# Lists of instruction order and PSUM banks in the place of a list scheduler, in an adaLN transformer block on one core

## The chip, the cores and the metric

The program is one transformer block with adaptive layer norm and runs on one core of a Trainium2 chip. Five engines of the core have queues of their own and run beside one another: TensorE (PE, matmuls; its weight loader is shown as PEld), VectorE (DVE), ScalarE (ACT), GpSimd (POOL), and SyncE (SP), which here only issues DMA transfers. An instruction runs when those ahead of it on its engine are done and the semaphores that it waits for have been raised. TensorE writes into PSUM, eight banks of 512 float32 values by 128 partitions; everything else lies in SBUF. The metric is the device time of one execution in microseconds (us), as the median of several runs.

## The reference

```python
x = A_x                                                # [1, 2048, 1024], bf16
sa, ca, ga, sb, cb, gb = split(_silu(c) @ w_mod, 6)    # w_mod [1024, 6144]
h = _layernorm(x) * (1 + ca) + sa
q = (h @ wq).reshape(1, 2048, 32, 32).transpose(0, 2, 1, 3)   # 32 heads of 32
k, v = h @ wk, h @ wv                                         # one k and one v, [1, 2048, 32]
p = _softmax(einsum('bhqd,bkd->bhqk', q, k) * 32 ** -0.5)
o = einsum('bhqk,bkd->bhqd', p, v)
x = x + ga * (merge_heads(o) @ wo)
h = _layernorm(x) * (1 + cb) + sb
x = x + gb * ((_silu(h @ w1) * (h @ w3)) @ w2)         # w1, w3 [1024, 3584], w2 [3584, 1024]
```

## The kernel before

**Work and stages.** The 2048 tokens are cut into 8 blocks of 256. A *unit* is one block with one group of four heads, so there are 64 units; each takes 8 *steps* over the keys, 256 keys a step, 512 steps in all. A step (`s_exp`, L1257) is one score group on TensorE, eight matmuls that use 32 rows of the array each (`S<-QT,KT`, the keys against the queries of four heads), into four of the six score banks S6 (banks 0 to 5), and two exponentials on ScalarE (`U<-S`), which write one slot of the ring U (10 slots). When a unit's eight steps are done, its 64 matmuls with V (`PB<-U,V`, `av`, L1355, with 32 columns of the array each) sum the values; VectorE adds the probabilities in pairs (`PS<-U`, `PS<-PS`), and a few matmuls with a matrix of ones (`PB<-PS,ONES`) turn these sums into the softmax denominators. The rest of TensorE's work uses the full array: the projections of q, k and v, the output product with wo, and the feed-forward network of each block.

**The feed-forward network.** A block has 14 *slabs* of 256 hidden columns (`slab`, L1495). A slab is two accumulation groups of 16 matmuls, one against w1 and one against w3; ScalarE evicts the first with a tanh into TS, VectorE makes the gated product from it and from the second into HHT. Each slab needs two loads of 512 KB, one of w1 and one of w3, which go into one of three slots (`W13SL`, `slab_dma`, L1480): slots 0 and 1 lie in the tile W, slot 2 in the tile HT, so the names `PB<-QT,W` and `PB<-QT,HT` say which slot a slab reads (and `S<-QT,W`, `S<-QT,HT` where its group stands in a score bank, see below). Then come four *quarters* (`quarter`, L1532) of w2, 56 matmuls each (`PB<-W2S,HT`), with a gated residual sum into X and a store. The network and the output product of block n run among the attention steps of block n+1; those of the last block run after the attention. The start of the program has the modulation vectors, the layer norm of the 16 token tiles (`ln_stats`, L1026; the tile ST takes the statistics, XN or XNB the normalised tile), k, v and the first q.

**What sets the order.** The kernel first writes down a graph: 7,193 nodes, each one operation or a small group of matmuls, made by `op` (L55) with what it reads and writes. Edges follow from these. (All instructions are replayed through one helper, so in the profile all have the line L22.) The accumulation groups are sessions (`Sess`, L25); each needs one PSUM bank from its first matmul until its last eviction. Two banks, 6 and 7, serve them during attention; the six score banks are added as they come free at the end (`later`).

`Placer` (L564) then schedules the graph. Again and again it takes, over all engines, the node that can start first by its own clock, which runs on the durations written in the graph. Among the nodes of an engine that could start within a small slack it takes the one with the least due time `vt`. To a due time it adds an offset by kind and engine; slack, offsets and a few switches stand in the table PLAN, one row for each 8 score groups. A session takes whichever bank comes free first. `emit` (L741) turns a node into instructions and gives it the semaphore waits that its edges need, leaving out those that an earlier wait implies.

The core of the choice:

```python
for st, n in cand:
    if st <= m + slack or (n.mode == "S" and st <= m + late):
        ...
        k = (n.vt + off.get(n.tag + "/" + n.alts[0][0] if n.tag else "", 0) + (1e5 if back else 0.0), st, n.i)
        if best is None or k < best[0]:
            best = (k, st, n)
```

Each engine's instructions leave in the order of this schedule. SP's loads too: a load of a slab waits on SP until the last matmul that reads its slot is done, and the loads behind it on SP wait with it.

Of the kernel before, what the change touches and what calls it, by code (L numbers as in the profile page):

```python
# [42 lines left out]
class Graph:  # L43
# [63 lines left out]
    def alias(self, new, old):  # L107
# [7 lines left out]
PLAN = [  # L115
    (0.15, 0.06, 0.0, 1, 2.5,
     {"-/pe": -103, "-/act": -50, "-/sp": 3, "an/dve": 282, "av/dve": -1, "k/pe": -256, "k/dve": -10, "kb/pe":
      -34, "kb/dve": 65, "ln/pe": -40, "ln/act": -38, "ln/dve": -35, "ln/pool": -168, "mc/dve": -131, "mc/sp":
      108, "mod/pe": 152, "mod/dve": -37, "out/sp": -203, "pair/dve": 33, "q/pe": -5, "q/dve": 85, "q/sp": 102,
      "quarter/pe": 283, "quarter/dve": -115, "quarter/sp": -6, "s/pe": -111, "s/act": 268, "slab/pe": -5,  # L120
      "slab/act": -109, "slab/dve": -124, "slab/sp": -92, "v/pe": 334, "v/dve": -2, "v/pool": 65, "wo/pool": 36,
      "wo/sp": 49}),
    (0.05, 0.0, 0.02, 1, 0.5,
     {"-/pe": -121, "-/dve": 5, "-/pool": 99, "an/dve": 28, "av/pe": -78, "av/dve": 293, "k/pe": -7, "k/dve": 5,
      "kb/pe": -3, "kb/dve": -7, "ln/pe": -135, "ln/act": -119, "ln/dve": 218, "ln/pool": 78, "mc/pe": -52,
      "mc/dve": -88, "mc/sp": 27, "mod/pe": -3, "mod/dve": -58, "pair/dve": 15, "q/pe": -194, "q/dve": 14,
      "quarter/dve": 169, "s/pe": -109, "s/act": 7, "sc/dve": -11, "slab/pe": -47, "slab/act": -3, "slab/dve":
      -201, "slab/sp": 35, "v/pe": 32, "v/dve": -164, "v/pool": 298, "wo/pe": -1, "wo/dve": 18, "wo/pool": 11,
      "wo/sp": 3}),
    (0.3, 0.16, 0.1, 0, 3.1,  # L130
     {"-/pe": -93, "-/act": 12, "-/dve": -31, "-/pool": -31, "an/dve": 150, "av/pe": 7, "av/dve": 140, "k/pe":
      32, "k/dve": 90, "kb/pe": 2, "kb/dve": -29, "ln/pe": -31, "ln/act": -6, "ln/dve": 351, "ln/pool": -30,
      "mc/pe": -4, "mc/dve": -69, "mc/sp": -137, "mod/dve": 45, "out/sp": -162, "pair/dve": 66, "q/dve": 67,
      "quarter/pe": -36, "quarter/sp": 1, "s/pe": -112, "s/act": 140, "sc/dve": -32, "slab/pe": 146, "slab/act":
      -146, "slab/dve": -120, "slab/sp": -5, "v/pe": 131, "v/pool": -72, "wo/dve": 100, "wo/pool": -3}),
    (0.12, 0.06, 0.3, 0, 3.0,
     {"-/pe": 23, "-/act": -86, "-/dve": -4, "an/dve": 63, "av/pe": -29, "av/dve": 40, "k/pe": 4, "kb/dve": -10,
      "ln/pe": -27, "ln/act": 2, "ln/pool": 220, "mc/pe": 152, "mc/dve": 120, "mc/sp": -35, "mod/pe": -220,
      "mod/dve": -16, "out/sp": -16, "q/dve": 7, "q/sp": -147, "quarter/pe": -153, "quarter/dve": -41,
      "quarter/sp": -39, "s/pe": 23, "s/act": 1, "sc/dve": 74, "slab/pe": -18, "slab/dve": 2, "slab/sp": 30,  # L140
      "v/pe": -5, "v/dve": 35, "v/pool": 168, "wo/pool": 2, "wo/sp": -85}),
    (0.12, 0.24, 0.1, 1, 0.8,
     {"-/pe": -90, "-/act": 54, "-/dve": -67, "-/pool": 131, "an/dve": 109, "av/pe": 17, "av/dve": -135,
      "k/dve": 56, "kb/dve": 4, "ln/pe": -27, "ln/act": 1, "ln/pool": -16, "mc/pe": 4, "mc/dve": 10, "mc/sp":
      -8, "mod/dve": -44, "out/sp": -171, "q/pe": -226, "q/dve": -34, "q/sp": -3, "quarter/pe": 37,
      "quarter/dve": 416, "quarter/sp": -122, "s/pe": 145, "s/act": 282, "sc/dve": -18, "slab/pe": 96,
      "slab/act": -104, "slab/dve": 17, "slab/sp": 60, "v/pool": 23, "wo/pe": -24, "wo/dve": -41, "wo/pool":
      -164, "wo/sp": -28}),
    (0.12, 0.2, 0.02, 1, 3.2,
     {"-/pe": 9, "-/act": 22, "-/dve": -30, "-/pool": 14, "an/dve": 85, "av/pe": -38, "av/dve": -130, "k/pe": 8,  # L150
      "k/dve": 63, "kb/dve": 1, "ln/pe": -5, "ln/act": 96, "ln/dve": 351, "ln/pool": -16, "mc/pe": -3, "mc/dve":
      -18, "mc/sp": -3, "mod/pe": 2, "mod/dve": -44, "out/sp": -301, "pair/dve": -20, "q/pe": -94, "q/dve": 65,
      "q/sp": -7, "quarter/pe": 74, "quarter/dve": 413, "quarter/sp": 5, "s/pe": 204, "s/act": 233, "sc/dve": 9,
      "slab/pe": 91, "slab/act": -185, "slab/dve": -46, "slab/sp": 109, "v/pe": -238, "v/pool": 21, "wo/pe":
      152, "wo/dve": -41, "wo/pool": -168}),
    (0.12, 0.24, 0.1, 1, 3.0,
     {"-/pe": -31, "-/act": -14, "-/dve": -102, "-/pool": 64, "an/dve": 82, "av/pe": -6, "av/dve": 45, "k/pe":
      8, "k/dve": -141, "kb/dve": 25, "ln/pe": 20, "ln/act": -6, "ln/dve": -26, "mc/pe": -24, "mc/dve": 11,
      "mc/sp": -1, "mod/dve": -323, "out/sp": -145, "pair/dve": -133, "q/pe": -377, "q/dve": 7, "q/sp": -120,
      "quarter/pe": -44, "quarter/dve": -73, "quarter/sp": 5, "s/pe": 253, "s/act": 174, "sc/dve": 14,  # L160
      "slab/pe": 160, "slab/act": -109, "slab/dve": -216, "v/pe": -127, "v/pool": 1, "wo/pe": 51, "wo/dve": 14,
      "wo/pool": 47, "wo/sp": -14}),
    (0.15, 0.1, 0.0, 0, 2.6,
     {"-/pe": -17, "-/act": -69, "-/dve": -18, "-/pool": 34, "-/sp": -218, "an/dve": -166, "av/pe": -66,
      "av/dve": -19, "k/dve": 2, "kb/pe": 5, "kb/dve": -14, "ln/pe": -2, "ln/act": 6, "ln/dve": -14, "mc/pe":
      -57, "mc/dve": -128, "mc/sp": 152, "mod/pe": 56, "mod/dve": -240, "out/sp": -39, "q/pe": -36, "q/dve":
      -159, "q/sp": -155, "quarter/pe": -28, "quarter/dve": -6, "s/pe": 272, "s/act": 34, "sc/dve": 14,
      "slab/pe": -98, "slab/act": -33, "slab/dve": 13, "slab/sp": 89, "v/pe": -96, "v/pool": 191, "wo/pe": 168,
      "wo/dve": -77, "wo/sp": -8}),
    (0.15, 0.03, 0.1, 1, 2.6,  # L170
     {"-/pe": -16, "-/act": -51, "-/dve": -18, "-/pool": -118, "-/sp": -70, "an/dve": -32, "av/pe": 65,
      "av/dve": -89, "k/pe": 8, "k/dve": -133, "kb/dve": 16, "ln/pe": 69, "ln/act": -29, "ln/dve": -47, "mc/pe":
      -167, "mc/dve": 12, "mc/sp": -82, "mod/pe": -87, "mod/dve": -293, "out/sp": -51, "pair/dve": 208, "q/pe":
      -17, "q/dve": -76, "q/sp": 22, "quarter/pe": -25, "quarter/dve": 30, "quarter/sp": 10, "s/pe": 357,
      "s/act": -68, "sc/dve": 36, "slab/pe": -3, "slab/act": -68, "slab/dve": -150, "slab/sp": 263, "v/pe": 178,
# [385 lines left out]
]  # L561


class Placer:  # L564

    SWITCH = {"F": 0.105, "S": 0.111, "A": 0.1155}
    LAT = {("dve", "pe"): 0.12, ("act", "pe"): 0.1, ("act", "dve"): 0.06}
    SEM = 0.06
    SPAN = 8
# [1164 lines left out]
```

## Time and profile before

| | |
|---|---|
| runs, us | 1131.63, 1131.49, 1130.08 (median 1131.49) |
| the profiled execution, span, us | 1129.6 |
| instructions in it | 34,462 |
| bytes moved by DMA | 209.45 MB, mean 185 GB/s |
| exponentials, busy us, mean of one | 1024, 961.7, 1154 ns |
| pair sums PS<-U on VectorE | 248, 300.9 us, 1218 ns |
| loads of w1 and w3, 512 KB each | 150 into W and 74 into HT, 5.0 us each to landing (median) |

The span runs from the first to the last instruction that the profiler recorded. The time of a run holds some launch work besides. Busy times of one engine can overlap in the records (an exponential's mean of 1154 ns is longer than the distance from one to the next), so the prediction counts from start to start where it needs a price.

In groups of the profile a line reads: engine, operation, output tile <- input tiles, partitions x elements, count; then busy us, mean ns, and idle time ahead of them with what ended it. A line of the waits reads: the waiting instruction, what released it, then the idle us, the count, and the longest one. In the timeline the two first numbers are start and duration in us, and a bracket at the end is idle time ahead of the group with its releaser. In the stretches each engine has its busy us and its number of instructions.

### The profile page before, as it was taken

The page shows a single profiled execution, that of the slowest core. Times are in us where ns is not written, and L with a number is a line of the kernel's source. Part 1 is how long each engine was busy: PE and PEld are TensorE (multiplying, and loading weights), DVE is VectorE, ACT ScalarE, POOL GpSimd, SP SyncE. Part 2 cuts the span into 40 slices and gives each one's busy share as a digit, 9 for nine tenths or more (in the row PEclk, how much of TensorE's full clock was granted, in tenths as well). Part 3 has the DMA queues.
Part 4 walks back from the last instruction along what each step waited for, and adds up shares of the span by engine and source line. Part 5 has one row for each costly group of instructions (what it writes and reads, how often), then busy time and mean ns, then how long its engine had stood idle before and what let it go on. Part 6 is the DMA issues. An engine that isn't in the chain of part 4 may idle for free.

```text
span 1129.6 us, 34462 instructions
## 1 busy us (share of the span) xinstructions
PE 1110.8 (98%) x15472; PEld 753.3 (67%) x15472; DVE 976.4 (86%) x1484; ACT 1017.2 (90%) x1155; POOL 51.5 (5%) x95
## 2 busy tenths in 40 slices
PE   8999999999999999999999999999999999999998
PEld 6643445666577766777577766776577756776887
DVE  7877899999899989998999899988999899987542
ACT  6899999999999999999999999999999999984110
POOL 4100000000000001000100001000100001000000
PEclk9999999999999999999999999999999999999999
DMA  9500368665697656865696577865597568677794
GB/s 345 184 2 2 113 184 225 192 183 164 141 245 203 190 141 179 243 192 155 151 269 192 166 184 179 237 193 155 129 274 207 157 172 209 195 223 217 222 249 154
DMA packets 374307, 209.45 MB, mean 185 GB/s; under 512 B 17552, under 2 KB 365968, under 8 KB 374160
## 3 DMA queue, kind: packets, MB, share of 16 engines
q1 hardware_dynamic: 373728, 207.11, 66.3%
q8 instruction: 122, 2.00, 0.8%
q14 instruction: 25, 0.20, 0.1%
q10 hardware_dynamic: 432, 0.13, 0.0%
HBM read 199.89 MB, written 4.19 MB: 181 GB/s over the span
## 4 chain that ended last, share of the span: by engine, by line
PE 73%; ACT 22%; DVE 2%; DMA 1%; issue 0%; SPq 0%; POOL 0%
PE PB L22 55%; ACT U L22 21%; PE S L22 19%; DMA W<-in_A_wq_dram 1%; ACT HT L22 1%; DVE ST L22 1%; DVE PS L22 1%; DVE HT L22 0%; SPq L22 0%; ACT XNB L22 0%; DVE KT L22 0%; DVE XNB L22 0%; POOL RS L22 0%; DVE QT L22 0%; DVE X L22 0%
## 5 line engine op out<-in xcount | busy, mean ns | idle before, releaser
L22 ACT ACTIVATE U<-S 128x1024 bf16<-128x1024 f32 x1024 | 961.7, 1154 | 7.2 <-PE S L22 5.1
L22 DVE TENSOR_TENSOR PS<-U 128x2048 bf16<-128x2048 bf16 x248 | 300.9, 1218 | 34.1 <-ACT U L22 30.9
L22 DVE TENSOR_TENSOR PS<-PS 128x1024 bf16<-128x1024 bf16 x304 | 268.3, 883 | 4.8
L22 PE MATMUL PB<-QT,W 128*128 128x256 bf16 x1824 | 226.7, 273 | 0.0
L22 PE MATMUL S<-QT,KT 32*128 32x256 bf16 x4096 | 203.7, 273 | 6.8 <-ACT U L22 3.3
L22 PEld LDWEIGHTS PB<-QT,W 128*128 128x128 bf16 x1824 | 167.5, 98 | 45.7 <-issue 27.6
L22 PE MATMUL PB<-W2S,HT 128*128 128x256 bf16 x1512 | 187.5, 273 | 0.0
L22 PEld LDWEIGHTS PB<-W2S,HT 128*128 128x128 bf16 x1512 | 138.2, 98 | 39.4 <-issue 23.6
L22 PEld LDWEIGHTS S<-QT,KT 32*128 32x128 bf16 x4096 | 60.8, 92 | 141.6 <-ACT U L22 137.7
L22 PE MATMUL PB<-U,V 128*32 128x256 bf16 x4096 | 132.3, 273 | 0.6 <-DVE QT L22 0.6
L22 PE MATMUL PB<-QT,HT 128*128 128x256 bf16 x928 | 117.0, 273 | 0.0
L22 PEld LDWEIGHTS PB<-U,V 128*32 128x32 bf16 x4096 | 105.7, 97 | 12.9 <-issue 8.0
L22 PE MATMUL PB<-HT,W 128*128 128x256 bf16 (+1 forms) x576 | 103.3, 320 | 1.1 <-DVE QT L22 0.5
L22 PEld LDWEIGHTS PB<-QT,HT 128*128 128x128 bf16 x928 | 85.4, 98 | 22.7 <-issue 13.3
L22 DVE SCALAR_TENSOR_TENSOR HT<-HT,PB 128x512 bf16<-128x512 bf16 x100 | 68.4, 684 | 18.0 <-ACT HT L22 17.6
L22 ACT ACTIVATE HT<-PB 128x512 bf16<-128x512 f32 (+1 forms) x102 | 71.4, 701 | 9.0 <-PE PB L22 8.2
L22 PEld LDWEIGHTS PB<-HT,W 128*128 128x128 bf16 x576 | 50.2, 98 | 38.8 <-issue 14.6
L22 DVE TENSOR_TENSOR HT<-HT,PB 128x512 bf16<-128x512 bf16 x100 | 68.2, 682 | 4.3 <-PE PB L22 3.1
L22 ACT ACTIVATE HT<-S 128x512 bf16<-128x512 f32 (+1 forms) x16 | 11.1, 702 | 59.7 <-PE S L22 59.6
L22 POOL TENSOR_SCALAR RS<-MV 128x1 f32<-128x1 f32 x32 | 14.2, 445 | 968.8 <-DVE MV L22 968.8
L22 PE MATMUL PB<-WO,QT 128*128 128x512 bf16 x224 | 55.4, 381 | 0.0
L22 PEld LDWEIGHTS PB<-WO,QT 128*128 128x128 bf16 x224 | 18.8, 97 | 24.6 <-issue 7.2
(119 smaller groups left out, 699.4 us busy)
## 6 DMA issues: line engine op xcount, KB each, us to landing
W<-in_B_w_dram SPq DMA_DIRECT2D x150, 512.0 KB, 5.0
W2S<-in_B_w_dram SPq DMA_DIRECT2D x28, 1792.0 KB, 8.3
HT<-in_B_w_dram SPq DMA_DIRECT2D x74, 512.0 KB, 5.0
W2S<-in_w_mod_dram SPq DMA_DIRECT2D x8, 1024.0 KB, 7.4
X<-in_A_x_dram SPq DMA_DIRECT2D x8, 512.0 KB, 6.6
out_dram<-X SPq DMA_DIRECT2D x7, 512.0 KB, 9.6
U<-in_B_w_dram SPq DMA_DIRECT2D x1, 3584.0 KB, 18.3
W2S<-in_B_w_dram SPq DMA_DIRECT2D x1, 3584.0 KB, 12.7
```

What stands on the lines that cost most here:

```text
L22: return getattr(e, call[0])(*call[1], **call[2])
```

## The change

The class `Placer` and the table PLAN go. In their place stand ORDER, which has for each of the five engines a list of all node numbers in the order in which they are to be issued, and BANKS, a string with one digit for each session, its PSUM bank, in the order in which the sessions are created in the graph. A class `Ordered` walks the five lists. It issues an engine's next node when all nodes that it depends on have been issued (issued in the walk, that is: this is no clock) and, for the first matmul of a session, when its bank has been given back. There are no costs, no due times and no choice left. The graph, its durations and due times, the emission of waits and the rest of the kernel are as before.

```diff
-PLAN = [
-    (0.15, 0.06, 0.0, 1, 2.5,
-     {"-/pe": -103, "-/act": -50, "-/sp": 3, "an/dve": 282, "av/dve": -1, "k/pe": -256, "k/dve": -10, "kb/pe":
...
-class Placer:
...
+    "pool": """
+        0-2 61-62 70 92 63 71-72 93 144 94 101-103 82 153 145 154 146 155 88 164-166 173-175 3 192 184 193 185 202-203
...
+BANKS = (
+    "7767776667767676667767676776776667676767676767676767676667766676776766777767667766766767777667667676"
...
+class Ordered:
+
+    def __init__(self, g, banks, later, order, bank_of):
...
+        self.order = {}
+        for e, text in order.items():
+            ids = self.order[e] = []
+            for t in text.split():
+                a, _, b = t.partition("-")
+                ids += range(int(a), int(b or a) + 1)
...
+        self.free = {b: () for b in banks}
+        self.later = dict(later)
+        self.bank_of = bank_of
 
     def run(self):
...
+        for s, b in zip(seen.values(), self.bank_of):
+            s.bank = int(b)
...
         while left:
...
+            for e, ids in self.order.items():
+                while at[e] < len(ids):
+                    n = nodes[ids[at[e]]]
+                    if not all(p.done for p in n.preds):
+                        break
+                    s = n.sess
+                    if s is not None and id(s) not in opened:
+                        if s.bank in self.later and all(u.done for u in self.later[s.bank]):
+                            self.free[s.bank] = tuple(self.later.pop(s.bank))
+                        prev = self.free.get(s.bank)
+                        if prev is None:
+                            break
+                        opened.add(id(s))
+                        self.free[s.bank] = None
+                        for p in prev:
+                            n.preds.setdefault(p, False)
+                        s.prev = prev
+                    at[e] += 1
...
+                    self.emit(n, e, next(f for a, f, _ in n.alts if a == e))
...
-    pl = Placer(G, (6, 7), later, PLAN)
+    pl = Ordered(G, (6, 7), later, ORDER, BANKS)
```

What the lists move shows in the two orders of instructions. At three places they read as follows, a line a run of like instructions with its output tile, its input tiles, its shape, and how many stand in a row.

SP at the start of the program, before the change: X and W2S take token tiles, U takes pieces of w_mod for the first two modulation vectors, W takes the first 512 KB of wq.

```order
L22 DMA X<-in_A_x_dram 128x2x1024 x2
L22 DMA U<-in_w_mod_dram 128x6x1024
L22 DMA X<-in_A_x_dram 128x2x1024
L22 DMA U<-in_w_mod_dram 128x2x1024
L22 DMA W2S<-in_A_x_dram 128x2x1024
L22 DMA W<-in_A_wq_dram 128x8x256
L22 DMA U<-in_w_mod_dram 128x6x1024
L22 DMA W2S<-in_A_x_dram 128x2x1024
```

SP at the start, after the change:

```order
L22 DMA X<-in_A_x_dram 128x2x1024 x3
L22 DMA U<-in_w_mod_dram 128x6x1024
L22 DMA U<-in_w_mod_dram 128x2x1024
L22 DMA W<-in_A_wq_dram 128x8x256
L22 DMA W2S<-in_A_x_dram 128x2x1024 x2
L22 DMA U<-in_w_mod_dram 128x6x1024
L22 DMA U<-in_w_mod_dram 128x2x1024
```

The third load of X now stands ahead of the first long load of w_mod, the load of wq ahead of the first token load of W2S, and the second token load of W2S ahead of the second long load of w_mod.

TensorE in the middle of attention, around the 266th of the 512 score groups (W2S with HT is a quarter of the network), before:

```order
L22 MATMUL S<-QT,KT 128x256 x8
L22 MATMUL PB<-PS,ONES 32x256 x4
L22 MATMUL PB<-U,V 32x256 x64
L22 MATMUL S<-QT,KT 128x256 x8
L22 MATMUL PB<-W2S,HT 128x256 x12
```

The same place after:

```order
L22 MATMUL S<-QT,KT 128x256 x8
L22 MATMUL PB<-PS,ONES 32x256 x4
L22 MATMUL PB<-U,V 32x256 x56
L22 MATMUL S<-QT,KT 128x256 x8
L22 MATMUL PB<-U,V 32x256 x8
L22 MATMUL PB<-W2S,HT 128x256 x10
```

Eight of the 64 matmuls of a unit's product with V have gone behind the next score group, and two matmuls of the quarter have gone on to a later gap.

TensorE in the tail, among the slabs of the last block (a slab is 16 matmuls for w1 and 16 for w3; HT is slot 2, W is slots 0 and 1), before:

```order
L22 MATMUL S<-QT,HT 128x256 x32
L22 MATMUL S<-QT,W 128x256 x64
L22 MATMUL PB<-QT,HT 128x256 x16
L22 MATMUL S<-QT,HT 128x256 x16
L22 MATMUL S<-QT,W 128x256 x64
L22 MATMUL S<-QT,HT 128x256 x16
L22 MATMUL PB<-QT,HT 128x256 x16
```

From the same part of the tail after:

```order
L22 MATMUL S<-QT,W 128x256 x4
L22 MATMUL S<-QT,HT 128x256 x6
L22 MATMUL S<-QT,W 128x256 x8
L22 MATMUL S<-QT,HT 128x256 x4
L22 MATMUL S<-QT,W 128x256 x8
L22 MATMUL PB<-W2S,HT 128x256 x2
L22 MATMUL S<-QT,W 128x256 x4
L22 MATMUL PB<-W2S,HT 128x256 x2
L22 MATMUL S<-QT,W 128x256 x16
L22 MATMUL PB<-W2S,HT 128x256 x2
L22 MATMUL S<-QT,W 128x256 x2
L22 MATMUL S<-QT,HT 128x256 x2
```

The slabs no longer follow one another whole: matmuls of two or three of them, and of the quarter of the block before, alternate in pieces of 2 to 16.

894 lines of the change are left out of this document (294 added, 600 removed).

## The prediction

> **What bounds the kernel now.** I read the profile's page first (engine shares, slices), then the stretches, then the waits and the timeline inside one stretch. TensorE and ScalarE are both nearly full:
>
> ```profile
> PE 1110.8 (98%) x15472; PEld 753.3 (67%) x15472; DVE 976.4 (86%) x1484; ACT 1017.2 (90%) x1155; POOL 51.5 (5%) x95
> PE   8999999999999999999999999999999999999998
> ACT  6899999999999999999999999999999999984110
> ```
>
> The same span cut into stages; the columns are busy us and counts of PE, PEld, DVE, ACT and POOL, then the granted clock, the DMA share and GB/s:
>
> ```profile
> 0.00:30.10 30.10, 24.91 (x356) 19.65 (x360) 22.60 (x55) 18.64 (x19) 14.65 (x41) 1.00 0.98 347
> 30.10:212.10 182.00, 174.89 (x2733) 92.47 (x2736) 158.20 (x276) 178.59 (x197) 7.49 (x15) 0.99 0.43 122
> 212.10:959.40 747.30, 744.26 (x10516) 506.64 (x10520) 691.41 (x995) 746.10 (x850) 27.76 (x36) 1.00 0.70 189
> 959.40:1028.00 68.60, 68.48 (x956) 50.18 (x957) 60.89 (x83) 64.31 (x75) 0.00 (x0) 1.00 0.68 193
> 1028.00:1054.00 26.00, 25.57 (x262) 19.41 (x261) 18.18 (x37) 1.22 (x2) 1.59 (x4) 1.00 0.84 240
> 1054.00:1102.00 48.00, 48.00 (x442) 43.01 (x441) 19.60 (x29) 8.36 (x14) 0.00 (x0) 1.00 0.98 255
> 1102.00:1129.60 27.60, 24.68 (x227) 21.89 (x224) 5.47 (x11) 0.00 (x0) 0.00 (x0) 1.00 0.46 149
> ```
>
> There are four regimes: a start limited by loads and layer norm; attention, in which both engines are full; from 1028 a tail in which ScalarE has little to do and TensorE never rests; and the last 27.6 us of one matrix product. How close both engines stand in attention comes from single rows. ScalarE around 500 us, then TensorE around 540:
>
> ```profile
> 498.47 5.73 ACT L22 ACTIVATE U<-S 128x1024 bf16<-128x1024 f32 x6
> 503.93 0.77 ACT L22 ACTIVATE HT<-PB 128x512 bf16<-128x512 f32 x1
> 504.40 3.96 ACT L22 ACTIVATE U<-S 128x1024 bf16<-128x1024 f32 x4
> ```
>
> ```profile
> 531.67 0.40 PE L22 MATMUL S<-QT,KT 32*128 32x256 bf16 x8
> 532.00 1.48 PE L22 MATMUL PB<-W2S,HT 128*128 128x256 bf16 x12
> 533.41 0.40 PE L22 MATMUL S<-QT,KT 32*128 32x256 bf16 x8
> ...
> 540.69 0.40 PE L22 MATMUL S<-QT,KT 32*128 32x256 bf16 x8
> 541.02 0.29 PE L22 MATMUL PB<-PS,ONES 128*32 128x256 bf16 x4
> 541.14 1.92 PE L22 MATMUL PB<-U,V 128*32 128x256 bf16 x64
> 542.99 0.40 PE L22 MATMUL S<-QT,KT 32*128 32x256 bf16 x8
> 543.32 1.48 PE L22 MATMUL PB<-W2S,HT 128*128 128x256 bf16 x12
> 544.74 0.40 PE L22 MATMUL S<-QT,KT 32*128 32x256 bf16 x8
> ```
>
> Start to start, six exponentials take 5.46 us (0.91 each) and a gate eviction 0.47. A full-array matmul of 256 columns takes 0.11 ((1.48 - 0.27) / 11, 0.27 being one matmul's own length). Going from the score groups' shape to the full array costs 0.33 - 0.22 = 0.11 (eight row-tiled matmuls run four abreast, two passes of 0.11), and back again 1.41 - 12 x 0.11 = about 0.1. I call such a change of shape a border, at 0.11.
>
> In the main stretch ScalarE owes 770 x 0.91 + 83 x 0.47 = 739.7 us of 747.3; its counts are these:
>
> ```profile
> L22 ACT ACTIVATE U<-S 128x1024 bf16<-128x1024 f32 x770 | 725.1, 1156 | 0.5
> L22 ACT ACTIVATE HT<-PB 128x512 bf16<-128x512 f32 x83 | 57.9, 698 | 0.7
> ```
>
> So no order, however good, takes more than 7.6 us out of this stretch. TensorE's side of it, in the waits of the same stretch:
>
> ```profile
> PEld S L22 <- ACT U L22: 96.5, 378, 0.6
> ```
>
> A border alone leaves the weight loader idle for some 0.21, as at 504 us (in brackets):
>
> ```profile
> 504.30 0.12 PEld L22 LDWEIGHTS S<-QT,KT 32*128 32x128 bf16 x8 [0.21 <-ACT U L22]
> ```
>
> So 378 x 0.21 = 79.4 of this is borders and 17.1 is real waiting for exponentials. TensorE's own demand is 747.3 - 17.1 = 730.2.
>
> **The change part by part.** Counted over both orders, not one instruction is added, removed or given to another engine, and five of six TensorE steps stay between the same two score groups; nearly all others move by one. The costs lie in four places.
>
> *Borders.* The old order has 1,071 changes of shape, the new one 1,111: 40 x 0.11 = 4.4 us more TensorE work, 27 of them (3.0 us) in the main stretch. There they first use up waiting: 730.2 + 3.0 = 733.2 is still under ScalarE's 739.7. Charged in full 3.0, hidden 0; I take half, 1.5, since both engines are within 2% of full and each stalls the other. The 13 others lie before 212 us, where ScalarE is short of nothing but TensorE's punctuality.
>
> *Main stretch.* What the borders buy is evenness. The step at 540.69 takes 2.30 us and its neighbour 1.75, against ScalarE's 1.82 (two exponentials). A product with V that stands whole in one gap (31 in the old order, 21 in the new) makes the next score group late, and ScalarE's loss isn't given back. Cut in two, the pair reads 2.08 (eight matmuls, 0.22, less) and 1.86 (these eight and a border more, two full-array matmuls fewer), each nearer to 1.82. Bounds: a gain of 7.6 (ScalarE never late) and a loss of 7.6 by symmetry (a worse order would have to lose as much again). I take a gain of 3.5, somewhat under half, because one third of the whole products are cut and the rest still stand; with the borders 2.0.
>
> *Start.* Loads move on SP: the first 512 KB of the query weights go one 512 KB load earlier, and two input loads go ahead of 1.5 MB. At 347 GB/s that is 1.5 us and over 4 us. VectorE waited for exactly these two, and for the shift column:
>
> ```profile
> DVE ST L22 <- DMA W2S<-in_A_x_dram: 1.0, 1, 1.0
> DVE PS L22 <- DMA W<-in_A_wq_dram: 1.0, 1, 1.0
> DVE SAB L22 <- PE S L22: 0.7, 1, 0.7
> ```
>
> All three lie on the chain before the first score group: a gain of 2.7 at most. Against it, VectorE now takes the statistics of the third token tile before it closes those of the first, and ScalarE's first normalisation slips by about three statistics and what follows them. The chain of the start has two of them in 1.19, and the first score group comes at 30.06:
>
> ```profile
> 19.16 1.19 DVE ST L22 x2
> ```
>
> ```profile
> 30.06 0.40 PE L22 MATMUL S<-QT,KT 32*128 32x256 bf16 x8
> ```
>
> Three at 0.6 are 1.8, at worst 1.5 of it in the open after what is saved. I take a gain of 1.0.
>
> *First attention stretch, 30 to 212 us.* ScalarE was busy for 178.6 of 182.0, so at most 3.4 can be had; the price of a loss is bounded by the 4.9 us that it already waits for score groups, and then by as much again. I take a gain of 1.0, the same share of its bound as above.
>
> ```profile
> ACT U L22 <- PE S L22: 4.9, 7, 2.0
> ```
>
> *Tail.* Each of the last block's 14 slabs needs two 512 KB weight loads into a ring of three slots. A load is issued when the slot's last reader is done. The old order reads slab after slab: of the 22 loads that wait for a reader, each has 80 to 88 matmuls (8.7 us and more) until its first reader. The new order mixes the slabs: 50 to 72 matmuls, seven times 50, or 5.45 us. What a load takes, in the first ten us and then in the rest of the tail (the number at the end is the median from issue to landing):
>
> ```profile
> W<-in_B_w_dram SPq DMA_DIRECT2D x4, 512.0 KB, 5.3
> HT<-in_B_w_dram SPq DMA_DIRECT2D x2, 512.0 KB, 4.5
> ...
> W<-in_B_w_dram SPq DMA_DIRECT2D x10, 512.0 KB, 6.2
> HT<-in_B_w_dram SPq DMA_DIRECT2D x6, 512.0 KB, 6.2
> ```
>
> At 6.2 plus some 0.2 for the issue, a load with 50 matmuls stops TensorE for 0.95. Three of the seven come early, where 4.5 to 5.3 fit; of the other four two lie in one another's shadow, so three stops, 2.8 us. TensorE is all of the time here (48.00 of 48.00), so nothing hides it. Bounds: 0 if every load takes 5.3 (5.5 against 5.45), and 7 x 0.95 plus 0.7 for the two just above 50, 7.4, if none shadows another. I take 2.8, as the medians of the later row are what those loads met.
>
> The Trainium skill bears on this price: "DMA: Bandwidth & Descriptors", section "Latency and other measured facts", gives HBM access as 0.2 us on average and 2 us at high load, with a smaller fixed cost when the load is lighter. The rows agree in kind (4.5 to 5.3 early, 6.2 later). By that rule the first stop thins out the requests, later loads come down to 5.3, and the tail would cost 0.95 instead of 2.8.
>
> *The end.* After the last matmul the kernel still does one eviction, one addition and one store; the new order ends in the same half of the last quarter, so 0.
>
> Sum: -2.0 main, -1.0 start, -1.0 first stretch, +2.8 tail = -1.2 on the span of 1129.6, which gives 1128.4. The median of the runs, 1131.49, lies 1.9 above the profiled span; I predict 1130.3.
>
> **The rivals.** *The tail loads land in time.* Were 5.3 to hold throughout, the tail costs nothing, and with it the sum is -4.0: 1127.5; with the main stretch at its best too (-7.6 + 1.5) 1123.4, and with the start at its best (-2.7) 1121.7. For it: loads of the same size took 4.5 and 5.3 in the same regime. Against it: sixteen later loads have 6.2 as their median, at the same pace of requests.
>
> *The tail decides: slower.* Place: 1054 to 1102. The new order needs loads back in 5.45, and the mix of slabs also brings two loads due almost together. If each shortened load costs its own stop, the tail costs 7.4, and the sum is +3.4: 1134.9; without the gain of the main stretch +5.4: 1136.9. It decides from a landing time of about 6.6 on, where seven stops of 1.35 with half of them shadowed already outweigh the 4.0 of gains. For it: nothing in the tail covers a stop. Against it: stops overlap, as one load's delay lengthens the others' time.
>
> *Nothing comes of evenness.* The new order has 3.0 us more TensorE work where TensorE has 17.1 of waiting; if ScalarE is late as often as before, at other steps, only the tail and the start remain: -1.0 + 2.8 + 1.5 = +3.3 at worst, +0.3 with the borders hidden and the first stretch unchanged but for half of its tail: about 1132.
>
> **How the numbers follow.** My sum holds with a chance of 0.33 (own range 1127 to 1133), loads in time 0.26, the tail decides 0.31, nothing from evenness 0.10. A change of 0.2% (2.3 us) is about what a measurement here tells from none: 1129.2 to 1133.8 counts as the same. My sum gives 0.11 faster, 0.20 same, 0.02 slower; loads in time 0.24 and 0.02 same; the tail 0.03 same and 0.28 slower; the last 0.08 same and 0.02 slower. That is 0.35 faster, 0.33 same, 0.32 slower. The range takes in the second case down to its best and the third up to 1136.9 with a little for its unknown size: 1121.7 to 1138.
>
> **What would show it.** Tail: in 1054 to 1102, stops of TensorE released by loads of W or HT, none before; 48.0 us become about 50.8. Main stretch: 770 exponentials in about 745 instead of 747.3, and the wait of PEld for U falls from 17.1 over its borders, whose count rises by 27. Start: the first score group at about 29 instead of 30.06, with the two load waits of VectorE gone. I am wrong if bank waits (TensorE for an eviction by VectorE), hardly there today, appear in the hundreds, since many accumulation groups now open on a bank soon after its last reader; or if main stretch and tail both move the other way.

## The result, and the profile after

| | median us | runs, us | |
|---|---|---|---|
| before | 1131.36 | 1130.08 to 1133.01, 21 runs | |
| changed | 1133.15 | 1131.97 to 1135.23, 20 runs, and one of 1229.79 | ratio 1.002, 95% interval 1.0013 to 1.0026 |

The run of 1229.79, at a granted clock of 0.85, is not in the ratio, and the old kernel's runs lie in two groups, nine up to 1130.35 us and twelve from 1131.24 on, which go with a clock of 1.0 and of 0.998 wherever the clock is listed.

The changed kernel is slower by 0.2%, 1.8 us. The sum had come out 1.2 us faster. The time lies in the stated range, but the likeliest case had the sign wrong, and none of the four cases describes what happened.

The profiled execution of the changed kernel has a span of 1133.4 and took 1135.23 in all, 2.1 above the median of its kernel, so its stages add up to more than the medians differ by. Its stages, with the same borders and columns as before:

```profile
0.00:30.10 30.10, 25.30 (x352) 21.29 (x352) 22.48 (x56) 18.28 (x19) 13.95 (x40) 0.89 0.99 346
30.10:212.10 182.00, 174.66 (x2738) 91.39 (x2738) 156.93 (x277) 179.55 (x197) 8.32 (x15) 1.00 0.40 118
212.10:959.40 747.30, 742.62 (x10471) 498.38 (x10472) 669.95 (x985) 745.24 (x847) 21.98 (x36) 1.00 0.71 187
1054.00:1102.00 48.00, 47.26 (x430) 41.46 (x428) 16.61 (x27) 6.95 (x12) 0.00 (x0) 1.00 0.89 249
1102.00:1133.40 31.40, 28.51 (x262) 25.31 (x259) 7.98 (x16) 1.19 (x2) 0.00 (x0) 1.00 0.44 141
```

In the same 747.3 us of the main stretch ScalarE issued 847 instructions instead of 850 (770 and 83 were the counts of exponentials and tanh in the prediction's view, whose window was 0.7 us wider), and TensorE 45 matmuls fewer. How far each kernel is ahead or behind shows best in the starts of the exponentials, read from the records one by one (us against the kernel before, which has them at 30.51, 212.51 and 960.81; the column "end" is the end of the last operation on PE, ACT or DVE; the star is explained below):

| | step 0 | step 96 | step 480 | end | 96 to 480 |
|---|---|---|---|---|---|
| changed * | +0.05 | -0.36 | +3.11 | +3.83 | **+3.5** |
| e1_start_new * | -0.38 | -1.11 | -1.12 | -1.12 | 0.0 |
| e2_main_new * | -0.03 | +0.45 | +3.87 | +4.79 | **+3.4** |
| e3_tail_new | -0.08 | -0.25 | -0.25 | -0.35 | 0.0 |
| e4_whole * | -0.30 | -0.91 | -0.40 | -0.42 | +0.5 |
| e5_mix | -0.39 | +0.15 | +44.85 | +45.76 | +44.7 |
| e6_lists * | -0.05 | +0.42 | +3.92 | +3.92 | +3.5 |
| e7_pe_old | -0.38 | +0.15 | +2.99 | +2.85 | +2.8 |
| e8_ends_new * | -0.65 | -1.36 | -1.38 | -1.69 | 0.0 |
| e9_short_old | +0.16 | +0.23 | -7.46 | -7.46 | -7.7 |
| e10_short_new * | -0.17 | -0.51 | +1.08 | +0.49 | +1.6 |
| e11_margin * | +2.89 | +1.53 | +0.54 | +1.87 | -1.0 |
| e12_middle * | +0.02 | -1.04 | -1.01 | -1.18 | 0.0 |

One thing in this table is not the order. In the profiled execution of the kernel before, the granted clock was half for 3.4 us within attention. Its row of these 3.4 us, and behind it the row of e2_main_new, which has the same order there and the full clock (same columns as above):

```profile
129.65:133.06 3.41, 3.41 (x26) 1.23 (x19) 2.45 (x7) 2.60 (x4) 0.00 (x0) 0.50 0.84 277
129.65:133.06 3.41, 3.35 (x32) 1.44 (x24) 3.36 (x8) 3.41 (x5) 0.00 (x0) 1.00 0.83 272
```

Up to step 52 e2_main_new and e6_lists are level with the kernel before, and from step 57 on they are 1.4 us ahead, with the same order. A star marks the kernels that had the full clock from step 0 to step 96. Against the old order at full clock, 1.4 us have to be added to their columns step 96, step 480 and end. The last column is free of this, but for e5_mix, which had two more such stretches there (2.8 us at the same price, an estimate). The changed kernel's half clock lies at the start, before the first step (0.89 in its first row).

Most of the loss arose between steps 96 and 480, where the prediction had put its largest gain: 3.5 us of 3.8, or of 5.2 with the 1.4 added. The waits of this stretch, first of the kernel before (its wait of PEld for U stands in the prediction), then of the changed one; columns are total us, count and the longest:

```profile
DVE PS L22 <- ACT U L22: 23.0, 28, 2.2
DVE HT L22 <- ACT HT L22: 12.6, 29, 1.1
DVE HT L22 <- PE PB L22: 4.9, 15, 1.2
PE PB L22 <- DVE HT L22: 0.5, 1, 0.5
PEld PB L22 <- DVE HT L22: 0.4, 2, 0.2
```

```profile
PEld S L22 <- ACT U L22: 57.8, 233, 0.6
DVE HT L22 <- PE PB L22: 33.2, 37, 2.8
DVE HT L22 <- ACT HT L22: 25.6, 37, 2.2
PEld PB L22 <- DVE HT L22: 4.9, 18, 0.6
DVE PS L22 <- ACT U L22: 2.8, 4, 1.1
PEld PB L22 <- DMA HT<-in_B_w_dram: 1.7, 3, 1.0
PE PB L22 <- DVE HT L22: 1.6, 6, 0.4
ACT U L22 <- PE S L22: 1.1, 3, 0.5
```

TensorE waits less for exponentials. In exchange it waits for VectorE's evictions, and VectorE, which used to run into its waits at the pair sums (23.0), now stands at the evictions of the slabs, waiting for TensorE (33.2 instead of 4.9) and for the tanh (25.6 instead of 12.6). The waits of PEld hold a border's 0.21 each, so I also counted from the starts on TensorE what is longer than matmuls and borders take. Waiting for exponentials fell from 9.6 to 2.2 us, waiting for VectorE rose from 0.7 to 8.4, and 1.3 for weight loads is new. With 27 borders more (2.9) and 0.8 less of small items that is +3.7, as measured between the score groups themselves (+3.5 by the exponentials).

One such wait, in the timeline, where slab 9 of the second block gives way to slab 10 (counted from 0); the changed kernel first, then the one before:

```profile
364.23 1.48 PE L22 MATMUL PB<-QT,HT 128*128 128x256 bf16 x12
365.54 0.64 ACT L22 ACTIVATE HT<-PB 128x512 bf16<-128x512 f32 x1
366.07 0.83 PE L22 MATMUL PB<-QT,HT 128*128 128x256 bf16 x6
366.20 0.69 DVE L22 SCALAR_TENSOR_TENSOR HT<-HT,PB 128x512 bf16<-128x512 bf16 x1 [0.60 <-ACT HT L22]
367.04 0.60 PE L22 MATMUL PB<-QT,W 128*128 128x256 bf16 x4
```

```profile
366.05 0.64 ACT L22 ACTIVATE HT<-PB 128x512 bf16<-128x512 f32 x1
366.58 1.70 PE L22 MATMUL PB<-QT,HT 128*128 128x256 bf16 x14
366.76 0.68 DVE L22 SCALAR_TENSOR_TENSOR HT<-HT,PB 128x512 bf16<-128x512 bf16 x1
368.12 0.60 PE L22 MATMUL PB<-QT,W 128*128 128x256 bf16 x4
```

In both, a group of w1 ends, ScalarE evicts it (tanh), VectorE multiplies, and then its bank is free. In the old order the other bank's group has 14 matmuls left: VectorE is done at 367.44, the bank is reopened at 368.12. In the new order the tanh starts at once and VectorE stands ready, so all is done at 366.89. But TensorE had only 6 matmuls left (0.66) and would have reopened at 366.73. It waits until 367.04. Over the stretch a bank is reopened after less than 1.5 us of TensorE's work in 58 of 261 cases (4 in the old order); 29 of the 58 follow a w3 group, 13 a product with V, and only 4 a w1 group like the one shown. And an eviction takes 1.34 us from the last matmul on the average, in both kernels. The Trainium skill, "Perfetto Trace Analysis", section "Matmuls", asks for independent groups to rotate through banks so that the evacuation of one overlaps the matmuls of the next; these traces agree, and put a length to it: 1.35 us for a w1 group and 0.72 for a w3 group where everyone stands ready.

### The profile page after: what moved, and what is told of

The parts are those of the page before. It is cut to its first block, busy times and chain, and to the rows that moved or that the text cites. A ratio compares the mean times of both kernels' runs of the same rounds, so it can differ in the third digit from the quotient of the medians.

```text
span 1133.4 us, 34406 instructions
## 1 busy us (share of the span) xinstructions
PE 1112.9 (98%) x15472; PEld 747.3 (66%) x15472; DVE 956.3 (84%) x1484; ACT 1020.3 (90%) x1155; POOL 46.0 (4%) x95
## 4 chain that ended last, share of the span: by engine, by line
PE 55%; ACT 37%; DVE 4%; DMA 3%; issue 1%; POOL 0%; SPq 0%; DVEq 0%
PE PB L22 40%; ACT U L22 34%; PE S L22 15%; ACT HT L22 2%; DVE PS L22 2%; DMA W<-in_B_w_dram 1%; DVE HT L22 1%; DVE ST L22 1%; DMA HT<-in_B_w_dram 1%; DMA QT<-XNB 0%; DVE X L22 0%; DMA X<-in_A_x_dram 0%; DVE QT L22 0%; DVE RB L22 0%; POOL RS L22 0%
## 5 line engine op out<-in xcount | busy, mean ns | idle before, releaser
L22 DVE TENSOR_TENSOR PS<-U 128x2048 bf16<-128x2048 bf16 x248 | 297.6, 1213 | 4.5 <-ACT U L22 2.8
L22 PE MATMUL PB<-QT,W 128*128 128x256 bf16 x1824 | 242.2, 273 | 1.6 <-DVE HT L22 0.6
L22 PEld LDWEIGHTS PB<-QT,W 128*128 128x128 bf16 x1824 | 165.1, 98 | 53.2 <-issue 31.1
L22 PE MATMUL PB<-W2S,HT 128*128 128x256 bf16 x1512 | 198.5, 273 | 0.0
L22 PEld LDWEIGHTS PB<-W2S,HT 128*128 128x128 bf16 x1512 | 136.4, 98 | 44.7 <-issue 27.4
L22 PE MATMUL PB<-U,V 128*32 128x256 bf16 x4096 | 137.2, 273 | 0.4 <-ACT U L22 0.3
L22 PE MATMUL PB<-QT,HT 128*128 128x256 bf16 x928 | 128.5, 273 | 1.3 <-DMA HT<-in_B_w_dram 1.0
L22 ACT ACTIVATE HT<-PB 128x512 bf16<-128x512 f32 (+1 forms) x102 | 64.5, 634 | 13.4 <-PE PB L22 12.8
L22 POOL TENSOR_SCALAR RS<-MV 128x1 f32<-128x1 f32 x32 | 8.4, 266 | 971.6 <-DVE MV L22 971.3
L22 PE MATMUL S<-QT,W 128*128 128x256 bf16 x256 | 36.0, 273 | 0.4 <-DMA W<-in_B_w_dram 0.3
```

The lines of the kernel that those rows point to most:

```text
L22: return getattr(e, call[0])(*call[1], **call[2])
```

## The experiments

**Which part of the program.** Three kernels use the new lists in one part only; they are cut at a score group, and each engine goes over from one list to the other there. As rows of the order (SP at the start, and TensorE behind the cut of the two others):

```diff
-DMA X<-in_A_x_dram 128x2x1024 x2
+DMA X<-in_A_x_dram 128x2x1024 x3
 DMA U<-in_w_mod_dram 128x6x1024
-DMA X<-in_A_x_dram 128x2x1024
 DMA U<-in_w_mod_dram 128x2x1024
...
```

> The lists of the changed kernel for everything up to the 96th score group, the old order behind it. By the two traces the 96th group comes 0.36 us earlier with the new lists, so 1131.0 against 1131.4. By the prediction's own terms (start -1.0, first attention stretch -1.0) it would be 1129.4. If neither term is real: 1131.4.

```diff
 MATMUL S<-QT,KT 128x256 x8
+MATMUL PB<-HT 128x256 x2
+MATMUL PB<-PS,ONES 32x256 x4
+MATMUL PB<-U,V 32x256 x16
+MATMUL S<-QT,KT 128x256 x8
+MATMUL PB<-U,V 32x256 x48
...
```

> The old order up to the 96th score group and from the 480th on, the new lists between. By the traces the stretch is 3.7 us longer, of which up to 2 may belong to the profiled execution alone (it was 2.1 above the median of its kernel): 1133.1 to 1135.1. By the prediction's term (-2.0) it would be 1129.4. If the loss sits elsewhere, 1131.4. On every theory that puts the loss into the banks, the waits of TensorE for an eviction by VectorE are there in full, some 8 us.

```diff
-MATMUL PB<-W2S,HT 128x256 x12
+MATMUL PB<-W2S,HT 128x256 x20
 MATMUL S<-QT,KT 128x256 x8
...
+MATMUL S<-WO,QT 128x512 x2
+MATMUL PB<-W2S,HT 128x256 x2
...
```

> The old order up to the 508th score group, the new lists behind it: the mixed slabs of the last block, whose loads have 50 to 72 matmuls instead of 80 to 88. The prediction's term is +2.8: 1134.2. The traces show only 0.2 more from the 511th group to the end: 1131.6. If loads land at very different times from run to run, the single times should spread more than those of the kernel before (1130.1 to 1133.0).

Measured: the start 1130.72 (ratio to before 0.9997, 0.9988 to 1.0006), the middle 1136.67 (1.0056, 1.0043 to 1.0068), the tail 1130.34 (0.9997, 0.9988 to 1.0005). The loss is in the middle. Its trace has +3.4 there, as the changed kernel's. It loses 1.9 more between steps 90 and 96 (1.4 of which the half clock hides in the table) and 0.9 behind the 480th step, where the lists are spliced; so its total overstates the middle. Start and tail alone can't be told from no change by their times. Their traces end 1.1 and 0.35 earlier, but e1_start_new is a starred row: with the 1.4 added it ends 0.3 later. Both ends together:

```diff
-DMA X<-in_A_x_dram 128x2x1024 x2
+DMA X<-in_A_x_dram 128x2x1024 x3
...
+MATMUL S<-WO,QT 128x512 x2
...
```

> The new lists up to the 96th score group and from the 508th on, the old ones between. The sum of what the two ends gave one by one in the traces, -1.1 and -0.1: 1130.2. If the ends' gains were noise: 1131.4.

1130.66 (0.9999, 0.9989 to 1.0008): again no change by the time, 1.7 us earlier by the trace, of which 1.4 are the half clock of the kernel before.

**Is it the banks?** e4_whole keeps the new gaps, borders and other lists, and takes the alternation of groups out of TensorE's list:

```diff
-MATMUL PB<-HT 128x256 x6
-MATMUL PB<-HT,W 128x256 x2
+MATMUL PB<-HT 128x256 x10
+MATMUL S<-QT,KT 128x256 x8
 MATMUL PB<-HT 128x256 x2
-MATMUL S<-QT,KT 128x256 x8
-MATMUL PB<-HT 128x256 x2
-MATMUL PB<-HT,W 128x256 x4
-MATMUL PB<-HT 128x256 x2
-MATMUL PB<-HT,W 128x256 x4
+MATMUL PB<-HT,W 128x256 x10
```

> The changed kernel, with one thing undone between the 96th and the 480th score group: in TensorE's list the full-array steps keep their places, but are filled session by session, each whole, in the order in which the new lists close them. Count and length of the gaps between score groups, the borders, and the lists of all other engines stay. A bank is then reopened at least 2.0 us of TensorE work after its last matmul in 251 of 261 cases instead of 140. Theory (the loss is bank turnaround): TensorE's waits for VectorE's evictions fall from about 8.4 us to about 1, the gain of the better placed tanh (3.8 us of ScalarE's idle time) stays, the time is 1126 to 1128.5. Rival A (score waits fell only because TensorE came late): the bank waits turn into waits for exponentials, about 1131. Rival B (the loss is the 27 added borders, 3 us): no change, 1133.

1131.86 (1.0005, 0.9997 to 1.0014): 1.3 under the changed kernel and no longer distinguishable from the old one. The stretch costs 0.5 instead of 3.5, so 3.0 of the loss came with the alternation. Waits for VectorE fell from 8.4 to 3.3; waits for exponentials rose from 2.2 to 5.3. So the time was nearer to rival A than to my theory, which had expected a gain over the old order. Rival B fell: the 27 borders are all still there. TensorE's waits for weight loads (1.3) went with the alternation too, so this run doesn't part the two; by ScalarE's idle time, below, the loads are the smaller part.

```profile
PEld S L22 <- ACT U L22: 66.0, 256, 0.9
PEld PB L22 <- DVE HT L22: 2.9, 12, 0.5
PE PB L22 <- DVE HT L22: 1.0, 4, 0.3
```

e5_mix is the reverse: the alternation alone, put into the old order.

```diff
-MATMUL PB<-HT 128x256 x12
-MATMUL PB<-HT,W 128x256 x6
+MATMUL PB<-HT 128x256 x6
+MATMUL PB<-HT,W 128x256 x2
+MATMUL PB<-HT 128x256 x4
+MATMUL PB<-HT,W 128x256 x4
+MATMUL PB<-HT 128x256 x2
```

> The kernel before, with one thing of the change put in between the 96th and the 480th score group: the full-array steps keep the old places (same gaps between score groups, same 794 borders), but are filled in the new lists' sequence, in which two accumulation groups alternate. All other engines keep the old lists. A bank is reopened within 1.5 us of TensorE work in 56 of 261 cases instead of 4. Theory (bank turnaround is the loss): TensorE's waits for VectorE's evictions rise from 1 us to 6 to 9, the stretch is 3 to 5 us longer, 1134 to 1136. Rival (TensorE has 10 us of waits for exponentials there, which the bank waits merely replace): 1131.4 to 1132.5.

1176.1 (1.0398, 1.0384 to 1.0412): ten times what I had expected. Rows of the same stretch:

```profile
DVE HT L22 <- PE PB L22: 67.6, 58, 3.5
ACT U L22 <- PE S L22: 24.8, 35, 2.6
PE PB L22 <- DVE HT L22: 24.2, 45, 1.9
ACT HT L22 <- PE PB L22: 10.5, 23, 1.6
```

I read these rows so: the alternation delays the end of each group a little. The old lists of ScalarE and VectorE expect that end earlier, and both take their instructions in order: while VectorE stands at one group's eviction (67.6 us), it can't free the other bank, and ScalarE standing at a tanh (10.5) issues no exponential. What cost 3 us in lists made for it costs 45 in others.

**The other engines' lists.** e6_lists has the old TensorE list and the new lists of the others in the middle, e7_pe_old the new lists everywhere but for the old TensorE list in the middle (rows of ScalarE and of TensorE):

```diff
-ACTIVATE U<-S 128x1024 x7
+ACTIVATE U<-S 128x1024 x8
 ACTIVATE HT<-PB 128x512
 ACTIVATE U<-S 128x1024 x5
...
```

> The kernel before, with the new lists of ScalarE, VectorE, SyncE and GpSimd between the 96th and the 480th score group, and the old list of TensorE throughout. If the tanh's place in ScalarE's list is what cut its idle time before tanh from 6.9 to 3.1 us, that gain is here without borders or bank waits: 1127.6 to 1130. If the lists fit only the new TensorE list (a tanh moved later delays its bank by 0.9 us), VectorE's evictions come later than TensorE reopens: 1132 or more. If the order on the other engines is indifferent: 1131.4.

```diff
-MATMUL PB<-HT 128x256 x2
-MATMUL PB<-PS,ONES 32x256 x4
-MATMUL PB<-U,V 32x256 x16
+MATMUL PB<-HT 128x256 x6
+MATMUL PB<-PS,ONES 32x256 x4
+MATMUL PB<-U,V 32x256 x24
...
```

> The changed kernel, with TensorE's list alone put back to the old one between the 96th and the 480th score group. Beside the kernel with whole accumulation groups (1131.9 measured) it has 27 borders fewer (3.0 us by 0.11 each) and the old places of the products with V (31 whole ones instead of 21). If the cut products bring the evenness that the prediction claimed (3.5 us): about 1132.4. If the borders cost and the cuts bring nothing: about 1128.9.

1135.68 (1.0043, 1.0031 to 1.0056) and 1133.73 (1.0024, 1.0014 to 1.0034). In the stretch, the new lists of the others lose 3.5 and 2.8 us under the old TensorE list (the total of e6_lists holds 1.9 more, lost just ahead of step 96 as in e2_main_new), with its 4 short reopenings and its 794 borders; the second branch of e6's expectation holds (a later tanh and a later eviction, bank waits of some 8 us). e7 came out over both its values: with 27 borders fewer it is 1.9 slower than e4_whole. So the borders are not the cost, and TensorE's new gaps are worth something, but only together with the new lists beside them.

**What bounds the stretch.** In e4_whole less waiting for banks had become more waiting for exponentials, as if ScalarE had no time to give. The timeline of ScalarE in the kernel before tells why:

```profile
569.16 0.60 ACT L22 ACTIVATE HT<-PB 128x512 bf16<-128x512 f32 x1
569.65 6.52 ACT L22 ACTIVATE U<-S 128x1024 bf16<-128x1024 f32 x7
575.98 0.68 ACT L22 ACTIVATE HT<-PB 128x512 bf16<-128x512 f32 x1
576.46 3.87 ACT L22 ACTIVATE U<-S 128x1024 bf16<-128x1024 f32 x4
```

By starts, seven exponentials take 575.98 - 569.65 = 6.33, 0.904 each. By ends, the first tanh ends at 569.76 and the seventh exponential at 576.17: 6.41, 0.916 each; the next four take (580.33 - 576.66) / 4 = 0.917. The recorded starts run ahead of the ends by 12.5 ns an instruction, until ScalarE really waits and the lead is gone. The end is what others wait for. Summed over all records with 0.917 for an exponential (0.914 behind a tanh) and 0.491 for a tanh, ScalarE owes 743.6 of the old order's 747.3 us and is idle for 3.5. In the changed kernel it is idle for 7.3, in e4_whole 4.4, in e6_lists 7.0, in e5_mix 48. Its work is the same in all of them, so its idle time must grow by what the stretch grows; this tells where the loss shows, not its cause. The cause shows in the places: ahead of exponentials ScalarE is idle for some 5.5 us in the changed kernel and 1.6 in the old one (all by ends). Of the 5.5, 2.2 stand at score groups with a wait of TensorE for VectorE in the gap just before or the one before that, and 0.7 at two with such a wait for a weight load; the rest is spread over short ones. In the old order none of the 1.6 stands at such a wait. The test of the bound is to make ScalarE's work shorter:

```diff
-                    U[:, c % NU, 2 * i:2 * i + 2, :, :].rearrange("p h k q -> p h (k q)"),
-                    S6[:, 2 * r[i]:2 * r[i] + 2, :], ACT.Exp, scale=SCALE)]
+                    U[:, c % NU, 2 * i:2 * i + 2, :, :].rearrange("p h k q -> p h (k q)")[:, :, 0:w],
+                    S6[:, 2 * r[i]:2 * r[i] + 2, 0:w], ACT.Exp, scale=SCALE)]
```

with `w = 504 if 96 <= c < 480 else 512`, in both kernels.

> The kernel before, with every exponential of the score steps 96 to 479 done on 504 of 512 columns of each bank (8 of 512 probabilities per row and bank are left as they were in the ring). By the records' ends an exponential takes 0.917 us for 1024 columns and a tanh 0.490 for 512, so 0.83 ns a column: 16 columns less are 13 ns, 10.2 us over 768 exponentials. Theory (ScalarE is the bound there: by ends it owes 743.6 of 747.3 us, idle 3.5): TensorE has 9.6 us of waits for exponentials, so the stretch gets 6.5 to 9.5 shorter, 1122 to 1125. Rival (the prediction's count, 739.7 owed and 7.6 idle, both engines limit each other): about half, 1126 to 1128. If ScalarE does not bound it: 1131.

> The changed kernel with the same shorter exponentials (504 of 512 columns in the steps 96 to 479). Theory (there TensorE's own work and its bank waits set the pace, and only 2.2 us of its waits are for exponentials): a gain of 2 to 4 against the changed kernel, 1129 to 1131, so that its distance to the old order grows from 1.8 to 6 or more. Rival (both orders are bound by ScalarE, and the change costs only what ScalarE waits for tanh and banks): the same gain as in the old order, 1124 to 1126.

The old order came to 1123.69 (0.9938, 0.9926 to 0.9951), 7.7 us less in the stretch, out of the 10.2 that ScalarE had less to do: for the most part ScalarE was the bound. The new order came to 1132.43 (1.0015, 1.0006 to 1.0024), outside my 1129 to 1131 and only 0.7 below the changed kernel (1.9 in the stretch by the traces, under my 2 to 4). With shorter exponentials the two orders are 8.7 us apart instead of 1.8. In the new order ScalarE's idle time rose to 16.1: there TensorE, with its bank waits, sets the pace. The rows of e9 and e10 in the stretch:

```profile
565.35 0.60 ACT L22 ACTIVATE HT<-PB 128x512 bf16<-128x512 f32 x1
565.84 6.42 ACT L22 ACTIVATE U<-S 128x1008 bf16<-128x1008 f32 x7
```

```profile
PEld S L22 <- ACT U L22: 42.4, 166, 0.6
DVE HT L22 <- PE PB L22: 34.1, 40, 2.8
PEld PB L22 <- DVE HT L22: 5.2, 18, 0.6
```

In e9 seven take (572.26 - 565.95) / 7 = 0.901 by ends. The Trainium skill, "ScalarE: Activation LUTs", section "What ACT_TABLE_LOAD costs", gives 0.833 ns a column and, for instructions with immediate operands back to back, 93 ns besides (186 less an overlap of 93): an estimate of 0.946 for 1024 columns. The slope agrees roughly (0.917 against 0.903 by the ends of all of e9's records, 0.88 ns a column); the sum is 0.917 here, and the measurement decides.

**Another order.** If the loss came from having no room, an order found with some room should keep its gain. I searched for two, by small moves, with starts and hand-over times from these traces.

```diff
-DMA SCC<-in_c_dram 128x8
 DMA PS<-in_A_wk_dram 128x256
 DMA PS<-in_A_wv_dram 128x256
+DMA SCC<-in_c_dram 128x8
...
```

> Another pair of lists, from small moves on the old order (TensorE, ScalarE and VectorE; SyncE's and GpSimd's lists stay), each kept only if the end came earlier by the starts, durations and hand-over times that the traces here show, and did so too with VectorE's results 0.02 to 0.05 us later and 0.5 to 2% longer, and weight loads 0.2 to 1.0 us later. By that reckoning the first score group comes 2.9 us earlier, the 96th 3.7, the 480th 5.2 and the end 7.0. Theory (an order loses where it has no room for what its reckoning doesn't know, and gains if it has some): 1124 to 1128. Rival (any order away from the old one loses its gain to bank waits as the changed one did): 1131 or more.

```diff
-ACTIVATE U<-S 128x1024 x7
-ACTIVATE HT<-PB 128x512
-ACTIVATE U<-S 128x1024 x5
+ACTIVATE U<-S 128x1024 x8
+ACTIVATE HT<-PB 128x512
+ACTIVATE U<-S 128x1024 x4
...
```

> The new lists up to about the 24th score group, the old lists from about the 505th on (SyncE's and GpSimd's lists old from the 96th), and between them an order found like that of e11_margin, but with VectorE's results 0.03 to 0.06 us later, its durations 1 to 3% longer and weight loads 0.4 to 0.6 us later as the further conditions. By that reckoning the end comes 2.8 to 3.5 us earlier than in the old order, 1.1 of it from the start (as e1_start_new had it). ScalarE's idle time between the 96th and the 480th group, 3.5 us by the records' ends in the old order, is all that can be had there. Theory: 1128 to 1130. Rival (every order away from the old one loses its gain to bank waits): 1131.5 or more.

e11 came to 1134.79 (1.0041, 1.0028 to 1.0055), a miss by 7 to 11 us. Its middle gained 1.0, not 1.5, and from step 480 on it lost 1.3. Above all, the first step came 2.9 later instead of 2.9 earlier: a load of c, moved two places back on ScalarE's queue, landed far later than reckoned, and ScalarE's first activation stood still for it, at 7.37 instead of 3.44. The order was not tried without this move.

```profile
7.37 0.21 ACT L22 ACTIVATE SCC<-SCC 128x8 bf16<-128x8 bf16 x1 [3.95 <-DMA SCC<-in_c_dram]
```

e12 leaves start and tail alone and came to 1130.5 (0.9997, 0.9988 to 1.0006). It is 1.0 ahead at step 96, less than the 1.4 of the half clock. Its middle was 0.9 ahead of e1 at step 416 and level with it at step 480. TensorE's waits for VectorE were 3.5 us there. So the rival's size of loss is not there, and the theory's gain isn't either; why the last 60 steps gave the gain back was not tried. Both orders also reopen banks soon, after less than 1.5 us of TensorE's work in 41 of 261 cases (e12) and 39 (e11), with 0.0 and -1.0 in the stretch, while e6_lists loses 3.5 with 4 such cases. So the count of short reopenings alone doesn't tell the loss. The waits that come of them do so better: 3.5 us in e12, 8.4 in the changed kernel. No kernel here with the whole work beats the old one by more than a measurement can tell.

## Why the prediction was wrong, point by point

*Main stretch (-2.0): the step that failed.* Three things in it. The bound was too wide: "no order, however good, takes more than 7.6 us out" rested on 0.91 an exponential, taken from start to start. By ends it is 0.917, and 3.5 us were to be had; by chance that is the number that I took as the expected gain. (The counts 770 and 83 also came from a window 0.7 us wider than the 747.3; inside it they are 768 and 82.) Second, TensorE's waits for exponentials fell as described, and more (9.6 to 2.2), but they were no loss of time: TensorE was early, with ScalarE full. ScalarE's idle time ahead of a tanh fell from 6.9 to 3.1 by starts, but by ends it is 1.6 in both kernels, so nothing was gained there. Third, and this made the loss, the reopening of banks was priced at nothing. It stood in the last paragraph as a sign of error, with "hundreds" for its count; dozens, 8.4 us, were enough. With the alternation taken out (e4_whole) these waits were 3.3 us and 3.0 of the 3.5 us of loss were gone.

*Borders (1.5 of 3.0 in the open).* The size was right, 2.9 measured. e4_whole, with all 27, loses 0.5 in the stretch, e6 and e7, without them, lose 3: most of it was hidden, as TensorE had 9.6 to spare. The prediction charged half.

*Start (-1.0).* The two load waits of VectorE are gone, as forecast, but ScalarE's first normalisation begins 2.5 later, where I had about 1.8:

```profile
7.89 1.22 ACT L22 ACTIVATE XNB<-X,NB,RS 128x1024 bf16<-128x1024 bf16 x1
```

```profile
10.40 2.37 ACT L22 ACTIVATE XNB<-X,NB,RS 128x1024 bf16<-128x1024 bf16 x2 [2.40 <-POOL NB L22]
```

The first score group came at +0.05 and, in e1, -0.4. Over the seven kernels with these lists at the start it came at -0.65 to +0.05, over the six with the old ones at -0.39 to +0.16: the gain of 1.0 is not there.

*First stretch (-1.0).* The table reads -0.4 from step 0 to step 96, and -0.7 in e1. That is less than the 1.4 which the half clock cost the kernel before. At full clock the new lists cost 1.0 here, 0.7 in e1, and 0.7 to 1.1 in e4, e8 and e10, so the sign was wrong. The clock of 0.99 in the prediction's row of this stretch was the sign of it, and most of the 1.4 was in the 3.4 us that the prediction thought could be had: from 120 to 142 us ScalarE is busy for 20.8 us in the kernel before and for all 22.0 in e2_main_new. What costs the 0.7 to 1.1 was not tried.

*Tail (+2.8).* It costs 0.7 from step 480 to the end in the changed kernel; with the same tail lists it gains 0.1 in e3, 0.0 in e4, 0.1 in e7, 0.3 in e8 and 0.6 in e10 from there. The rival "loads in time" was right on this. The term was mis-sized by the landing time: 6.2 was taken from the old order, and with the new one the same loads landed sooner. From 1064.3 us on:

```profile
W<-in_B_w_dram SPq DMA_DIRECT2D x9, 512.0 KB, 5.5
HT<-in_B_w_dram SPq DMA_DIRECT2D x5, 512.0 KB, 5.2
```

The stops that I had priced at 0.95 came to these in the whole tail, each wait counted on PE and on its loader:

```profile
PEld S L22 <- DMA W<-in_B_w_dram: 0.9, 2, 0.6
PEld PB L22 <- DMA W<-in_B_w_dram: 0.6, 1, 0.6
PE PB L22 <- DMA W<-in_B_w_dram: 0.4, 1, 0.4
```

This goes with the order: in the tail the medians are 4.9 to 5.6 in all six kernels with the new lists there and 6.0 to 6.6 in the eight others. Why the loads were faster was not tried; the mean rate from 1054 to 1102 us doesn't tell it (249 GB/s in the changed kernel, 276 in e4_whole, 255 in the old one). *The end (0)* was right.

Evenness was the wrong measure, since it looks at the gaps of one list. e6, e7 and e5 show that each half of the change, put into the other order, is about as bad as the change itself (3.5 and 2.8) or far worse (44.7).

## What to carry to other kernels

Take the period of an instruction from the ends of its records, over a run between two waits; 0.91 in the place of 0.917 for an exponential, and 0.47 in the place of 0.491 for a tanh, made 3.5 us of room look like 7.6. Where an engine is that full, first ask of an order what it does to the hand-overs around it: how much work lies between the last matmul of a group and the next one in its bank, against what the eviction takes with its queue. Short distances alone did no harm in e12, where the waits for evictions stayed at 3.5 us. Before two traces are compared step by step, compare their granted clocks stage by stage. And treat the lists of several in-order engines as one thing: a part of one order inside another is no small change.

## What was not expected of the hardware

ScalarE's recorded starts run ahead of its ends by 12.5 ns an exponential, up to some 0.3 us, and fall back at the next wait, which costs no time at the ends as long as the lead covers it (durations of like exponentials run from 1.02 to 1.35 us in one kernel). Mean durations in a view of groups therefore tell how seldom an engine waits (1156 ns in the old order's main stretch, 1061 in the new one's), not how long its work is.

The half clock came in pieces of 3.4 or 6.8 us. All seven kernels with the new lists at the start had one that began between 11.75 and 14.36 us, ahead of the first score group. Those with other lists at the start had none there; four of them (the kernel before, e3, e5 and e9) had one of 3.4 us at about 129 us, within attention, where it cost the kernel before 1.4 us. What brings it on was not tried.
